# The gated stage of a fused attention, expert and gated-product kernel: other places for the next block's transposes, sums and low parts, and another order of the output's sums

## Chip, cores and metric

The kernel runs on one NeuronCore of a Trainium2 chip, in one launch. The metric is the device time of that launch in microseconds (us); the time before is the median of three runs.

## What is computed

The reference is linear attention, then a mixture of experts with one expert for each token, then a gated product. Cut to what matters here:

```python
q_s = softmax(q, axis=-1); k_s = softmax(k, axis=2)
x = einsum('bhsd,bhde->bhse', q_s, einsum('bhsd,bhse->bhde', k_s, v))     # 4608 tokens x 512
y = gate_w * (relu(x @ w1[e]) @ w2[e])                                   # e = argmax of the gate, for each token
a = y @ w_a                                                              # 512 x 1536
b = y @ w_b                                                              # 512 x 1536
out = (a * b) @ w_out                                                    # 1536 x 512
```

The change lies in the last three lines alone, the gated stage.

## The kernel before

**Blocks, f and steps.** The gated stage takes the 4608 tokens in nine blocks of 512. In a block, a loop runs over `f` = 0 to 11 (128 columns of `w_a` and of `w_b` each). Both products are done at once by a scheme of seven products in place of eight (Strassen's, in Winograd's form), with every operand as a float16 high part and a float16 low part. So `step` (L1792) has seven *steps* for each `f`, and a block has 84, numbered k = 0 to 83. In each step TensorE (PE) first makes one of the products p1, p2, p6, p7, p5, p4, p3 (six matmuls, L1644) into one of two PSUM banks, `x` or `y`, in turn; the banks change their names with each `f`. Then follows one *chunk* of the output product (three matmuls, L1659), taken from a queue (`product()` in `step`).

**Who empties the banks.** p1, p6 and p7 are copied out by ScalarE (ACT; L1803, L1809, L1812). p2, p5 and p4 are added up by VectorE (DVE; L1806, L1815, L1818), p4 is followed by the product `g[:, 1]` (L1819, here *g1*), and p3 is read by the product `g[:, 0]` (L1822, here *g0*). A product can start when the one two steps before has been read out of its bank. From g0 and g1 come the operands of the output product: high parts by ACT (`hi`, L1681), low parts by DVE (`lo`, L1686), sums by GpSimd (POOL; L1695 to L1717). POOL also scales output weights (`scaled`, L1678), twice for each pair of `f`, after every sixth chunk.

**The next block, beside.** While a block is computed, `rows` (L1764) lists by step what is done for the next one: its rows are loaded (step 27, L1306), their peaks are found (`peak`, DVE, L1312), scaled (ACT, L1323), transposed in four *turns* (four PE transposes into the bank that is free, L1328, and one ACT copy out of it, `turned`, L1331), and then made into seven operands A11, A12, A22, S1 to S4: sums by DVE in halves (`add`, L1338), high parts by ACT (L835), low parts by DVE in halves (`lo`, L1348). Where a turn stands, one or two chunks of later steps are done early, so that PE has work while ACT copies.

**The last block's output.** The sums that make the output of the block before (`sum`, L1729) run in steps 1 to 26 of a block: DVE adds the PSUM accumulators p6, p7, p4, p5, p2, p3 one after the other (L1736). The accumulator of p3 is that of p5, which is added to: the chunks of p3 start in step 12.

**Order.** All is written out by hand: each engine takes its instructions in the order in which `step` issues them, which within a step is product, its reader, turn and `turned`, chunks, the operands' `tasks`, the output's `total`, and last what `rows` has put there (`late`).

Of the kernel before, what the change touches and what calls it, by code (L numbers as in the profile page):

```python
# [12 lines left out]
AF = mybir.ActivationFunctionType  # L13
# [23 lines left out]
class Attention:  # L37
# [70 lines left out]
    def rows(self, u):  # L108
        r = 64 * (u // 2 % 2)
        return slice(r, r + 64)  # L110
# [367 lines left out]
def setup_consts(tc, ctx, c):  # L478

    nc = tc.nc  # L480
    cp = ctx.enter_context(tc.tile_pool(name="const", bufs=1))
    c.ident = cp.tile([P, P], F32, name="ident")
    make_identity(nc, c.ident)
    c.two = cp.tile([P, P], F32, name="two")
    nc.gpsimd.memset(c.two, 2.0)
    c.plan = cp.tile([P, 3 * MAXSLOT + 2 * NE + 1], I32, name="plan")
    c.cand = cp.tile([P, 1], I32, name="cand")
    c.pick = cp.tile([P, MAXSLOT, NE], F32, name="pick")
    c.gidx = cp.tile([P, 2 * MAXSLOT], I32, name="gidx")
    c.carry = cp.tile([P, NE], F32, name="carry")  # L490
    nc.gpsimd.memset(c.carry, 0.0)
    c.first = cp.tile([P, NE], F32, name="first")

    def iota(name, n, step=1, base=0):
        t = cp.tile([P, n], F32, name=name)
        nc.gpsimd.iota(t, [[step, n]], base=base, channel_multiplier=0, allow_small_or_imprecise_dtypes=True)
        return t

    c.iota50 = iota("iota50", 2 * MAXSLOT)
    c.is1000 = iota("is1000", 4, base=-1000)  # L500
    c.w8 = iota("w8", NE, -1, NE)
    c.e8 = iota("e8", NE)
# [271 lines left out]
class Work:  # L774
# [20 lines left out]
    def step(self, flush=False):  # L795
        self.now += 1
        for e in self.room:
            self.room[e] = min(self.room[e] + self.STEP, self.STEP)
        for ch in list(self.chains):
            while ch[1] is not None:  # L800
                eng, cost, wait, *cond = ch[1]
                if self.now < ch[2] + wait or (cond and not cond[0]()) or (self.room[eng] < self.LEAST and not flush):
                    break
                self.room[eng] -= cost
                ch[1:] = next(ch[0], None), self.now
            if ch[1] is None:
                self.chains.remove(ch)
# [548 lines left out]
class Gated:  # L1356
# [372 lines left out]
    def sum(self, n):  # L1729

        nc, v, acc, b = self.nc, self.nc.vector, self.acc, self.y[n]
        u = [self.y1.rearrange("p t d -> p (t d)")[:, 512 * i:512 * i + 512].rearrange("p (t c) -> p t c", t=2)
             for i in range(4)]

        def add(o, x, nm, t):
            v.tensor_tensor(u[o][:, t], u[x][:, t], acc[nm][:, t], ALU.add)  # L1736

        def copy(t):
            nc.scalar.copy(u[0][:, t], acc["p1"][:, t])

        def store(t):
            ob = self.ob[t % 2]
            for k in range(2):
                nc.scalar.activation(ob[:, 256 * k:256 * k + 256], u[2 * (t // 2) + k][:, t % 2], AF.Copy, scale=b.fc[:, t:t + 1])
            put = nc.gpsimd.indirect_dma_start(out=self.o[:, :], in_=ob, in_offset=None,
                                               out_offset=bass.IndirectOffsetOnAxis(ap=b.id[:, t:t + 1], axis=0),
                                               bounds_check=NTOK - 1, oob_is_err=False)
            self.tc.declare_no_dep(put.ins, group="out", reason="no two rows have the same token")
            self.tc.add_to_no_dep_group("out", put.ins)

        do = {}
        for f, a, ks in ((copy, (), (1, 2)), (add, (1, 0, "p6"), (6, 7)), (add, (3, 1, "p7"), (8, 8)),
                         (add, (2, 3, "p4"), (10, 10)), (add, (3, 3, "p5"), (11, 11)),
                         (add, (0, 0, "p2"), (17, 21)), (add, (1, 1, "p3"), (23, 24))):
            for t in range(2):
                do.setdefault(ks[t], []).append((f, *a, t))
        for t, k in ((2, 16), (3, 18), (0, 25), (1, 26)):
            do.setdefault(k, []).append((store, t))
        for k in range(27):
            for f, *a in do.get(k, ()):  # L1760
                f(*a)
            yield

    def rows(self, n):  # L1764


        nc, b = self.nc, Rows(self, n, self.y1)
        self.y[n] = b
        late = {}

        def put(s, f, *a):
            late.setdefault(s, []).append(lambda: f(*a))

        put(27, b.load)
        for i, k in enumerate((33, 33, 34, 35, 35, 36, 37, 38)):
            put(k, b.peak, i // 2, slice(i % 2, i % 2 + 1))
        put(39, b.power)
        for t in range(4):
            put(39 + t, b.scale, t)
        turns = {44 + 7 * i: i for i in range(4)}  # L1780
        for j, adds, hi, *lo in ((self.A11, (), 53, 55, 56), (self.S3, (52, 53), 55, 57, 59), (self.A12, (), 67, 68, 69),
                                 (self.A22, (), 68, 70, 71), (self.S1, (66, 67), 69, 71, 72),
                                 (self.S2, (68, 69), 71, 73, 74), (self.S4, (70, 72), 74, 76, 77)):
            for k, at in enumerate(adds):
                put(at, b.add, j, slice(k, k + 1))
            put(hi, b.hi, j, nc.scalar)
            for k in range(2):
                put(lo[k], b.lo, j, slice(k, k + 1))
        put(80, b.factor)
        return b, late, turns  # L1790

    def step(self, n, f, beside):  # L1792


        nc, v = self.nc, self.nc.vector
        a, r, w, u = self.tmp
        g, cf = self.g[f % 2], self.cf[:, f:f + 1]
        i = f // 2
        first = self.A12 if f % 2 else self.A11
        x, y = (t[:, 0:256] for t in (self.banks[f % 2], self.banks[1 - f % 2]))  # L1800

        def p1():
            nc.scalar.copy(w, x)  # L1803

        def p2():
            v.tensor_tensor(a, w, y, ALU.add)  # L1806

        def p6():
            nc.scalar.copy(r, x)  # L1809

        def p7():
            nc.scalar.copy(w, y)  # L1812

        def p5():
            v.tensor_tensor(u, w, x, ALU.add)  # L1815

        def p4():
            v.tensor_tensor(r, r, y, ALU.add)  # L1818
            v.scalar_tensor_tensor(g[:, 1], r, cf, u, ALU.mult, ALU.mult)  # L1819

        def p3():
            v.scalar_tensor_tensor(g[:, 0], x, cf, a, ALU.mult, ALU.mult)  # L1822
            self.hi(i, first, g[:, 0])

        def product():
            next(self.queue, lambda: None)()

        b, late, turns = beside
        for k, use in enumerate((p1, p2, p6, p7, p5, p4, p3)):
            ps = y if k % 2 else x  # L1830
            k += 7 * f
            self.product(n, f, use.__name__, ps)
            use()
            if k in turns:
                b.turn(turns[k], self.banks[1 - f % 2])
                b.turned(turns[k])
                product()
                if f % 2:
                    product()
            if k - 1 not in turns and not (f % 2 and k - 3 in turns):  # L1840
                product()
            next(self.tasks, None)
            next(self.total, None)
            for do in late.get(k, ()):
                do()
# [102 lines left out]
```

## Time and profile before

| | |
|---|---|
| median of the runs | 1457.78 us (1457.41 to 1458.32, 3 runs) |
| the profiled execution: its own time, its span | 1467.53 us, 1465.8 us |
| PE busy | 1366.1 us, 93% of the span |
| DVE busy | 1043.0 us, 71% |
| ACT busy | 674.0 us, 46% |
| POOL busy | 564.2 us, 38% |
| granted TensorE clock, mean over the span | 0.976 |

Shares of busy time are means over the whole kernel, of which the gated stage is the second half, from 652 us on. A busy PE is not PE at its peak, since matmuls overlap and their ends are modelled. The profiled execution took 1467.53 us, 9.75 us more than the median of the runs that were timed without a profile.

### The profile page before, as it was taken

Reading aid. Unit: us, or ns where it says so; the run is one execution under the profiler, and the core shown is the slowest. Engines: PE = TensorE matmul, PEld = TensorE weight load, DVE = VectorE, ACT = ScalarE, POOL = GpSimd, SP = SyncE. Lnnn points to the kernel's source line nnn. Section 1 sums busy time; section 2 is a strip of 40 time slices with the busy share of each in tenths; the row PEclk is TensorE's granted clock in tenths of the full one; section 3 lists DMA queues with packets and bytes.
Section 4 is the critical chain, followed back from the end, with each engine's and each line's share of the span. In section 5 each row is a group of like instructions: output and inputs, shape, how many; then the busy total and the mean of one; then the engine's idle time right before and its main releaser. Section 6 shows DMA issues by size and latency. Waiting matters only on the chain.

```text
span 1465.8 us, 29137 instructions
## 1 busy us (share of the span) xinstructions
PE 1366.1 (93%) x11068; PEld 1112.0 (76%) x11068; DVE 1043.0 (71%) x2340; ACT 674.0 (46%) x1625; POOL 564.2 (38%) x698
## 2 busy tenths in 40 slices
PE   6887898998999999989999999999999999999996
PEld 4776775665576676768888888888888888888885
DVE  5889875875687776426767867777777777767764
ACT  4556554753455454324444444444444444444432
POOL 6755521523334354104343343433334333343433
PEclk9988798999999999999999999999999999999998
DMA  9998245788564345126010010100101001010000
GB/s 240 253 251 220 73 131 164 268 291 271 184 220 140 113 135 165 48 72 255 2 56 4 1 59 1 59 1 16 45 1 59 2 18 42 1 59 1 31 1 30
DMA packets 87919, 145.87 MB, mean 100 GB/s; under 512 B 19792, under 2 KB 60752, under 8 KB 85584
## 3 DMA queue, kind: packets, MB, share of 16 engines
q1 hardware_dynamic: 81136, 123.85, 26.8%
q0 software_dynamic: 6080, 19.95, 4.2%
q8 instruction: 92, 1.51, 0.5%
q14 instruction: 67, 0.55, 0.1%
q10 hardware_dynamic: 544, 0.02, 0.0%
HBM read 149.78 MB, written 46.44 MB: 134 GB/s over the span
## 4 chain that ended last, share of the span: by engine, by line
PE 41%; DVE 10%; issue 2%; ACT 1%; POOL 1%; POOLq 0%; DVEq 0%; ACTq 0%
PE ab L1644 27%; PE mp L1659 13%; DVE raw L1348 1%; DVE y L1338 1%; DVE gp L1686 1%; DVE w L1348 1%; PE ab L1328 1%; DVE ysb L1818 1%; DVE w L1819 1%; DVE xg L1806 1%; DVE g L1819 1%; DVE gu L1815 0%; DVE w L1822 0%; DVE g L1822 0%; DVE y L1736 0%
## 5 line engine op out<-in xcount | busy, mean ns | idle before, releaser
L1644 PEld LDWEIGHTS <-gw 128*128 128x128 f16 x3780 | 369.2, 98 | 60.0 <-issue 13.6
L1644 PE MATMUL ab<-raw,gw 128*128 128x256 f16 x2100 | 280.2, 272 | 5.6 <-ACTq L1267 2.7
L1644 PE MATMUL ab<-w,gw 128*128 128x256 f16 x1680 | 225.2, 273 | 0.8
L1659 PEld LDWEIGHTS <-gp 128*128 128x128 f16 x1944 | 190.8, 98 | 25.9 <-ACT gp L1681 2.1
L1061 PEld LDWEIGHTS <-w 128*128 128x128 f16 x1824 | 180.1, 99 | 38.6 <-issue 12.7
L1061 PE MATMUL ph<-xhl,w 128*128 128x256 f16 x1728 | 198.2, 276 | 9.7 <-issue 4.1
L1078 PE MATMUL py<-w,hh 128*128 128x512 f16 x576 | 172.5, 381 | 2.4 <-DMA w<-wd 2.4
L1659 PE MATMUL mp<-wo,gp 128*128 128x256 f16 x756 | 142.6, 273 | 0.0
L1686 DVE SCALAR_TENSOR_TENSOR gp<-gp,gs 128x256 f16<-128x256 f16 x162 | 81.1, 505 | 59.0 <-ACT gp L1681 58.0
L1069 DVE SCALAR_TENSOR_TENSOR hl<-ph,hh 128x256 f16<-128x256 f32 x144 | 59.2, 420 | 78.7 <-ACT hh L1068 75.6
L1078 PE MATMUL py<-w,hl 128*128 128x512 f16 x288 | 109.9, 382 | 0.0
L1078 PEld LDWEIGHTS <-hh 128*128 128x128 f16 x608 | 59.8, 99 | 64.7 <-issue 4.2
L1460 POOL TENSOR_TENSOR gf<-gf 128x256 f32<-128x256 f32 x72 | 64.5, 916 | 100.4 <-ACT gf L1503 92.0
L1681 ACT ACTIVATE gp<-g 128x256 f16<-128x256 f32 x108 | 45.0, 417 | 115.7 <-DVE g L1822 114.8
L1644 PEld LDWEIGHTS <-w 128*128 128x128 f16 x756 | 73.7, 97 | 29.5 <-issue 21.0
L1717 POOL TENSOR_TENSOR gs<-w 128x256 f32<-128x256 f32 x54 | 39.5, 732 | 134.0 <-DVE w L1822 134.0
L1681 ACT ACTIVATE gp<-w 128x256 f16<-128x256 f32 x54 | 22.5, 417 | 148.9 <-DVE w L1822 146.2
L1659 PE MATMUL mp<-raw,gp 128*128 128x256 f16 x324 | 88.6, 273 | 0.9 <-DVE gp L1686 0.9
L1659 PE MATMUL mp<-w,gp 128*128 128x256 f16 x324 | 88.8, 274 | 0.0
L1068 ACT ACTIVATE hh<-ph 128x256 f16<-128x256 f32 x144 | 54.0, 378 | 74.9 <-PE ph L1061 74.5
L1023 POOL DMA_INDIRECT xg<-xd,gidx x40 | 43.9, 1098 | 106.9 <-ACT xhl L1052 51.4
L1815 DVE TENSOR_TENSOR gu<-tables,ab 128x256 f32<-128x256 f32 x108 | 45.3, 419 | 54.2 <-PE ab L1644 47.1
(337 smaller groups left out, 2798.8 us busy)
## 6 DMA issues: line engine op xcount, KB each, us to landing
w<-wd SPq DMA_DIRECT2D x58, 1024.0 KB
raw<-in_moe_w_dram SPq DMA_DIRECT2D x24, 512.0 KB
yd<-ysb SPq DMA_DIRECT2D x19, 513.0 KB
xd<-x SPq DMA_DIRECT2D x8, 1026.0 KB
y<-yd SPq DMA_DIRECT2D x8, 1026.0 KB
w<-in_k_dram SPq DMA_DIRECT2D x16, 512.0 KB
wd<-wst SPq DMA_DIRECT2D x16, 512.0 KB
g<-in_moe_w_a_dram SPq DMA_DIRECT2D x12, 512.0 KB
```

What stands on the lines that cost most here:

```text
L1023: nc.gpsimd.indirect_dma_start(out=self.x[:, j], out_offset=None, in_=self.xd[0:4 * S if s == 0 else NTOK, :], in_offset=bass.IndirectOffs ...
L1061: nc.tensor.matmul(ph, self.w1[:, w, k, o], x[:, k], start=i == 0, stop=i == 11)
L1068: nc.scalar.activation(self.hh[:, f], ph, AF.Relu)
L1069: nc.vector.scalar_tensor_tensor(self.hl[:, f], ph, 0.0, self.hh[:, f], ALU.max, ALU.subtract)
L1078: nc.tensor.matmul(self.py[j], h[:, f, o], self.w2[:, w, f], start=f == 0 and i == 0, stop=f == 7 and i == 2)
L1460: self.nc.gpsimd.tensor_tensor(s[:, dst], s[:, x], s[:, y], ALU.subtract)
L1644: self.nc.tensor.matmul(ps, self.w[f][:, b, o:o + P], self.y[n].op[:, a, yl, 256 * k:256 * k + 256], start=i == 0 and fresh, stop=i == 5, ...
L1659: self.nc.tensor.matmul(self.acc[nm][:, t], x, y, start=i == t == j == 0 and nm != "p3", stop=i == last and t == 1 and j == 2, skip_group_ ...
L1681: self.nc.scalar.activation(self.part(i, a)[:, 0], x, AF.Copy, scale=2.0 ** -11)
L1686: eng.scalar_tensor_tensor(p[:, 1], p[:, 0], -2048.0, x, ALU.mult, ALU.add)
L1717: pool.tensor_tensor(x, a11, a21, ALU.subtract)
L1815: v.tensor_tensor(u, w, x, ALU.add)
```

## The change

Three tables of step numbers and one order are changed; the same instructions are issued, except that they stand elsewhere. Turns 0 to 3 stand at steps 44, 48, 51, 55 (before 44, 51, 58, 65), and the number of chunks done early beside them is now listed by step. The eight peaks take steps 32 to 38 one or two at a time. The next block's sums, high and low parts take steps 50 to 78 (before 52 to 77, most of them 66 to 77). In the output's sums p5 is added before p4, in step 9, and p4's two halves in steps 11 and 13; the two buffers that hold these results change places in `store`.

```diff
@@ sum
+        c = (u[0], u[1]), (u[3], u[2])
...
-                nc.scalar.activation(ob[:, 256 * k:256 * k + 256], u[2 * (t // 2) + k][:, t % 2], AF.Copy, scale=b.fc[:, t:t + 1])
+                nc.scalar.activation(ob[:, 256 * k:256 * k + 256], c[t // 2][k][:, t % 2], AF.Copy, scale=b.fc[:, t:t + 1])
...
-                         (add, (2, 3, "p4"), (10, 10)), (add, (3, 3, "p5"), (11, 11)),
+                         (add, (2, 3, "p5"), (9, 9)), (add, (3, 3, "p4"), (11, 13)),
@@ rows
-        for i, k in enumerate((33, 33, 34, 35, 35, 36, 37, 38)):
+        for i, k in enumerate((32, 34, 35, 36, 37, 37, 38, 38)):
...
-        turns = {44 + 7 * i: i for i in range(4)}
-        for j, adds, hi, *lo in ((self.A11, (), 53, 55, 56), (self.S3, (52, 53), 55, 57, 59), (self.A12, (), 67, 68, 69),
-                                 (self.A22, (), 68, 70, 71), (self.S1, (66, 67), 69, 71, 72),
-                                 (self.S2, (68, 69), 71, 73, 74), (self.S4, (70, 72), 74, 76, 77)):
+        turns = {44: 0, 48: 1, 51: 2, 55: 3}
+        for j, adds, hi, *lo in ((self.A11, (), 50, 51, 52), (self.S3, (50, 51), 52, 53, 55), (self.A12, (), 57, 58, 59),
+                                 (self.A22, (), 58, 63, 64), (self.S1, (60, 62), 63, 66, 67),
+                                 (self.S2, (65, 65), 66, 70, 72), (self.S4, (69, 73), 74, 77, 78)):
@@ step
+        more, less = ({44: 1, 48: 1, 51: 2, 55: 2}, (45, 49, 52, 54, 56, 58)) if turns else ({}, ())
...
-                product()
-                if f % 2:
+                for _ in range(more[k]):
                     product()
-            if k - 1 not in turns and not (f % 2 and k - 3 in turns):
+            if k not in less:
                 product()
```

In the rows of the changed kernel below, line numbers stand one or two higher (L1736 is L1737, L1803 is L1804), since lines were added above them.

ACT's order in steps 47 to 51, first before and then with the change. `tables` and `ysb` are the copies of p7, p1 and p6, `gs_12767<-gs` is the high part of S4, `gp_12766<-w_92` that of A11, which reads g0; `y_12761<-ab` is the copy that ends a turn, and L835 a high part of the next block.

```order
L1812 COPY tables<-ab_12771 128x256
L1681 ACTIVATE gs_12767<-gs 128x256
L1681 ACTIVATE gp_12766<-w_92 128x256
L1803 COPY tables<-ab_12771 128x256
L1809 COPY ysb<-ab_12771 128x256
L1331 COPY y_12761<-ab_12770 128x4x128
```

```order
L1813 COPY tables<-ab_12771 128x256
L1681 ACTIVATE gs_12767<-gs 128x256
L1681 ACTIVATE gp_12766<-w_92 128x256
L1331 COPY y_12761<-ab_12771 128x4x128
L1804 COPY tables<-ab_12771 128x256
L835 ACTIVATE w_91<-y_12761 128x512
L1810 COPY ysb<-ab_12771 128x256
L1331 COPY y_12761<-ab_12770 128x4x128
```

Turn 1 used to be copied after p6's copy (L1809) in step 51. Now its copy stands in step 48, right behind the high part that reads g0, and turn 2 has the place in step 51.

DVE's order in steps 69 to 74, before and then with the change. L1338 is a half sum of the next block, L1348 a half low part, L1686 a low part of this block's operands; L1822 is g0, L1806 the sum with p2, L1815 the sum with p5.

```order
L1348 TENSOR_TENSOR raw_90<-y_12761,raw_90 128x256
L1338 TENSOR_TENSOR y_12761<-y_12761 128x2x128
L1822 SCALAR_TENSOR_TENSOR g_12763<-ab_12771,gcf,xg 128x256
L1348 TENSOR_TENSOR raw_90<-y_12761,raw_90 128x256
L1338 TENSOR_TENSOR y_12761<-y_12761 128x2x128
L1686 SCALAR_TENSOR_TENSOR gp_12765<-gp_12765,g_12763 128x256
L1348 TENSOR_TENSOR raw_90<-y_12761,raw_90 128x256
L1338 TENSOR_TENSOR y_12761<-y_12761 128x2x128
L1806 TENSOR_TENSOR xg<-tables,ab_12771 128x256
L1686 SCALAR_TENSOR_TENSOR gp_12765<-gp_12765,g_12763 128x256
L1348 TENSOR_TENSOR raw_90<-y_12761,raw_90 128x256 x2
L1686 SCALAR_TENSOR_TENSOR gp_12765<-gp_12765,gs 128x256
```

```order
L1823 SCALAR_TENSOR_TENSOR g_12763<-ab_12771,gcf,xg 128x256
L1338 TENSOR_TENSOR y_12761<-y_12761 128x2x128
L1686 SCALAR_TENSOR_TENSOR gp_12765<-gp_12765,g_12763 128x256
L1348 TENSOR_TENSOR raw_90<-y_12761,raw_90 128x256
L1807 TENSOR_TENSOR xg<-tables,ab_12771 128x256
L1686 SCALAR_TENSOR_TENSOR gp_12765<-gp_12765,g_12763 128x256
L1686 SCALAR_TENSOR_TENSOR gp_12765<-gp_12765,gs 128x256
L1348 TENSOR_TENSOR raw_90<-y_12761,raw_90 128x256
L1686 SCALAR_TENSOR_TENSOR gp_12765<-gp_12765,gs 128x256
```

Between g0 (L1822) and the sum with p2 (L1806) stood five instructions, four of them for the next block and one for this; now there are three, two of them for the next block. Ahead of g0, too, stood two for the next block, and now none.

DVE's order in steps 8 to 12, before and then with the change. L1736 adds an accumulator to the output: `mp7` is p7, `mp4` p4, `mp5` p5.

```order
L1736 TENSOR_TENSOR y1_12761<-y1_12761,mp7_12773 128x256 x2
L1686 SCALAR_TENSOR_TENSOR gp0_12765<-gp0_12765,gs_12764 128x256
L1736 TENSOR_TENSOR y1_12761<-y1_12761,mp4_12775 128x256 x2
L1815 TENSOR_TENSOR gu_12762<-tables_119,ab1_12771 128x256
L1736 TENSOR_TENSOR y1_12761<-y1_12761,mp5_12777 128x256 x2
L1818 TENSOR_TENSOR ysb_94<-ysb_94,ab0_12770 128x256
```

```order
L1737 TENSOR_TENSOR y1_12761<-y1_12761,mp7_12773 128x256 x2
L1737 TENSOR_TENSOR y1_12761<-y1_12761,mp5_12777 128x256 x2
L1686 SCALAR_TENSOR_TENSOR gp0_12765<-gp0_12765,gs_12764 128x256
L1816 TENSOR_TENSOR gu_12762<-tables_119,ab1_12771 128x256
L1737 TENSOR_TENSOR y1_12761<-y1_12761,mp4_12775 128x256
L1819 TENSOR_TENSOR ysb_94<-ysb_94,ab0_12770 128x256
```

Both sums of p5 now stand right behind those of p7, ahead of the low part of step 10 (L1686), and only one half of p4 is left ahead of the sum with p4's product (L1818, now L1819).

## Rows read from the trace of the kernel before

**Rows 1.** Busy us of PE, PEld, DVE, ACT, POOL, then PEclk, DMA; two stretches.
```profile
1002.80:1091.70 88.90, 86.41 (x775) 75.60 (x773) 66.00 (x151) 39.41 (x103) 32.95 (x40) 1.00 0.08 25
...
1075.20:1084.20 9.00, 7.41 (x64) 6.05 (x63) 8.96 (x22) 4.33 (x11) 3.21 (x4) 1.00 0.01 2
```

**Rows 2.** Timeline, steps 11 and 12: start, us, instruction [idle before, releaser].
```profile
1014.74 0.82 PE L1644 MATMUL ab<-raw,gw 128*128 128x256 f16 x6
...
1015.00 0.83 POOL L1678 TENSOR_SCALAR w<-wo 128x768 f16<-128x768 f16 x1 [3.36 <-PE mp L1659]
1015.02 0.74 DVE L1736 TENSOR_TENSOR y<-y,mp 128x256 f32<-128x256 f32 x2
...
1015.82 0.38 PE L1659 MATMUL mp<-wo,gs 128*128 128x256 f16 x2 [0.26 <-DVE y L1736]
```

**Rows 3.** Timeline, steps 33 to 36 of the fifth block.
```profile
1036.65 0.42 DVE L1818 TENSOR_TENSOR ysb<-ysb,ab 128x256 f32<-128x256 f32 x1 [0.49 <-PE ab L1644]
...
1036.78 0.82 PE L1644 MATMUL ab<-raw,gw 128*128 128x256 f16 x6
...
1037.76 0.82 PE L1644 MATMUL ab<-raw,gw 128*128 128x256 f16 x6
...
1037.85 0.74 DVE L1312 TENSOR_REDUCE yh<-y 128x1 f32<-128x256 f32 x2
...
1038.50 0.48 DVE L1822 SCALAR_TENSOR_TENSOR w<-ab,gcf,xg 128x256 f32<-128x256 f32 x1
...
1039.03 0.82 PE L1644 MATMUL ab<-raw,gw 128*128 128x256 f16 x6
```

**Rows 4.** Timeline, where steps 70, 71, 76 and 80 begin, and one DVE row.
```profile
1075.23 0.82 PE L1644 MATMUL ab<-raw,w 128*128 128x256 f16 x6
...
1077.04 0.81 PE L1644 MATMUL ab<-raw,w 128*128 128x256 f16 x6 [0.67 <-DVE g L1822]
...
1078.39 1.04 DVE L1338 TENSOR_TENSOR y<-y 128x256 f32<-128x256 f32 x1
...
1083.36 0.81 PE L1644 MATMUL ab<-raw,w 128*128 128x256 f16 x6 [0.44 <-DVE gu L1815]
...
1087.76 0.81 PE L1644 MATMUL ab<-raw,w 128*128 128x256 f16 x6 [0.32 <-DVE xg L1806]
```

**Rows 5.** Timeline, the turns in steps 51 and 58 of the fifth block.
```profile
1055.38 0.60 PE L1328 MATMUL ab<-ident,y 128*128 128x128 f32 x4
...
1056.02 0.59 ACT L1331 COPY y<-ab 128x512 f32<-128x512 f32 x1
...
1062.04 0.82 PE L1644 MATMUL ab<-raw,gw 128*128 128x256 f16 x6
...
1064.32 1.14 PE L1644 MATMUL ab<-raw,gw 128*128 128x256 f16 x9
```

**Rows 6.** Timeline, steps 48 to 50 of the fifth block.
```profile
1051.61 0.82 PE L1644 MATMUL ab<-raw,gw 128*128 128x256 f16 x6
1051.86 0.83 POOL L1678 TENSOR_SCALAR w<-wo 128x768 f16<-128x768 f16 x1 [2.53 <-PE mp L1659]
1051.94 1.02 DVE L1819 SCALAR_TENSOR_TENSOR w<-ysb,gcf,gu 128x256 f32<-128x256 f32 x1
...
1052.89 0.41 DVE L1686 SCALAR_TENSOR_TENSOR gs<-gs,gs 128x256 f16<-128x256 f16 x1
1053.22 0.47 DVE L1822 SCALAR_TENSOR_TENSOR w<-ab,gcf,xg 128x256 f32<-128x256 f32 x1
...
1053.72 0.42 ACT L1681 ACTIVATE gp<-w 128x256 f16<-128x256 f32 x1 [3.19 <-DVE w L1822]
...
1053.74 0.81 PE L1644 MATMUL ab<-raw,gw 128*128 128x256 f16 x6
```

**Rows 7.** Timeline of SP: the load of the next block's rows is issued.
```profile
1029.81 0.33 SPq L1306 DMA_DIRECT2D y<-yd  x1
```

**Rows 8.** SP's waits in that block: for whom, us in total, times, longest.
```profile
SPq L1306 <- DMA y<-yd: 6.3, 1, 6.3
```

**Rows 9.** Columns as in rows 1: two stretches at the kernel's end.
```profile
1442.40:1445.80 3.40, 1.16 (x10) 0.56 (x7) 2.87 (x4) 1.89 (x7) 2.74 (x4) 1.00 0.00 0
1445.90:1449.20 3.30, 3.22 (x16) 2.31 (x17) 1.86 (x6) 0.19 (x1) 0.83 (x1) 0.50 0.00 0
```

**Rows 10.** Timeline of PE, where the last block's chunks of p3 begin.
```profile
1450.99 0.38 PE L1659 MATMUL mp<-wo,gs 128*128 128x256 f16 x2 [0.85 <-DVE y L1736]
```

## The prediction

> **What bounds it now.** I looked first at the granted clock, then at busy time by stretch, then walked the timeline of the fifth block (1002.78 to 1091.70 us; the second to eighth blocks repeat it to within some 10 ns a step). Over the block PE is busy for 86.41 of 88.90 us at full clock [rows 1]: the stage is a train of products and chunks on PE, and it can only gain where that train halts. A step that nothing delays takes 0.98 us, as from 1036.78 to 1037.76 [rows 3], which is nine matmuls 0.109 apart: 0.655 for the product, 0.33 for the chunk. 84 steps would take 82.5 us; four turns of four transposes add 4 x 0.44. So about 4.6 us a block are halts of PE, and the timeline shows where each stands:
>
> - Step 12, 0.42: its chunk is the first of p3 and adds to the accumulator of p5. It begins at 1015.82, released by DVE's sum (L1736), where the product before it began at 1014.74 and leaves PE free at 1015.40 [rows 2].
> - Steps 35 to 37, 0.29 + 0.17: two peaks (0.74 together) stand ahead of g0, which ends at 1038.98; the next product starts at 1039.03 in place of 1038.74 [rows 3]. A further one delays step 38 likewise.
> - Steps 70 to 80: from 1075.23 to 1087.76 are 12.53 us for ten steps, 9.83 undisturbed, so 2.70 lost; each halt ends with DVE [rows 4], and DVE is busy for 8.96 of 9.00 us there while PE is not [rows 1].
> - Step 58, 0.53: from 1062.04 to 1064.32 are 2.28 [rows 5], while product, transposes and two chunks need 0.655 + 0.44 + 0.655 = 1.75.
> - Step 49, 0.17: p1 to p2 would take 0.98 from 1052.59 and ends only at 1053.74 [rows 6].
> - The turn in step 51 has three chunks beside it: its transposes start at 1055.38, PE has work until 1055.38 + 0.44 + 0.98 = 1056.80, and the copy ends at 1056.61 [rows 5], so nothing is lost. Small halts in steps 7 and 44 make up the rest; the change leaves them as they are.
>
> **The output's sums.** p5 is now summed before p4. DVE has by then ended p7's sums; two sums take 0.74 [rows 2] and fill a stretch in which DVE waits, so p5 is read about 1.9 us earlier than now, well before 1015.40. The p4 halves go into steps 11 and 13, one at a time (0.41), inside the 0.6 us by which DVE's step work may be late. I take the whole 0.42, in each of eight blocks. In the tail PE idles 0.85 for the same sum [rows 10]; behind it stand stores that wait for others, so I count 0.5 there (0 to 0.85).
>
> **The peaks.** The first one moves to step 32, and there the load decides: issued at 1029.81 + 0.33 and waited for 6.3 us by SP's own wait [rows 7, 8], it has landed at 1036.44. DVE would start this peak at about 1036.1, so it now waits, and r + y (L1818, nominally 1036.65 [rows 3]) stands behind it and ends some 0.2 later. The product that waits for r + y starts at 1037.76, so there are 0.5 us left. Behind it g1, a low part and g0 (0.48 + 0.41 + 0.48) end near 1038.5, in time for 1038.74. I allow 0.2 more for the loads of other blocks, which still fits. Then no step has more peaks than its gap holds: 0.46 gained, with 0 and 0.46 as bounds.
>
> **The next block's sums and low parts.** Of its 22 half operations, ten stand now in steps 70 to 79, and five with the change; the rest go to steps 50 to 69, where DVE has room. Walking DVE's queue with the durations of the rows (0.41 for a half beside nothing, 0.95 to 1.04 where a POOL copy runs [rows 4, 6], each 0.08 overlapped), I find two narrow places, steps 61 and 64, and one miss of 0.05. So 2.70 are gained but for 0.1; the other bound is that each of the POOL copies met on the way pushes a reader beyond its slack, 1.2 a block.
>
> What the timeline shows of such a meeting: g1 (L1819) starts at 1051.94, just after POOL's scaling at 1051.86, and takes 1.02 in place of 0.48 [rows 6]; two sums that read PSUM take 0.74 beside the scaling of their step [rows 2], no more than two peaks without one [rows 3]. The Trainium skill (SBUF — State Buffer, Who interferes with whom) says that a VectorE instruction with two inputs in SBUF contends with a GpSimd instruction that reads SBUF, and that reductions never do; by it every moved sum and low part is exposed, and no peak. The trace agrees where it shows both.
>
> **The turns.** Turn 2 takes the place of turn 1 in step 51 and waits as little. The halt of 0.53 at step 58 and the 0.17 at step 49 go. But turns 1 and 3 now stand in steps 48 and 55, each behind p3, and ACT, which takes its instructions in order, has the high part that reads g0 ahead of the turn's copy.
>
> Step 48: p3 starts at 1051.61, the transposes can follow at 1052.27 and two chunks after them, so PE is ready for step 49's p1 at 1051.61 + 0.655 + 0.44 + 0.655 = 1053.36. That p1 writes the bank that the copy empties. g1 meets the scaling and ends at 1052.96, the low part and g0 follow until 1053.69, the high part until 1054.14 [rows 6]; the copy takes 0.59 [rows 5], overlapped by 0.08, and ends near 1054.65. p1 starts at 1054.70: a new wait of 1.33 (1.29 to 1.4 by the overlap; if g1 didn't meet the scaling, 0.79).
>
> Step 55: r + y ends 0.62 into the step (in [rows 3] it ends at 1037.07, 0.29 after p3's start at 1036.78 with a chunk of 0.33 between p4 and p3, and step 54 has no chunk); then g1 0.48, g0 0.47, high part 0.42, copy 0.59, less overlaps: 2.53 after p3's start. PE needs 0.655 + 0.44 + 0.98 = 2.08. A new wait of 0.45.
>
> **Sum for a block.** 0.42 + 0.46 + (2.70 - 0.1) + 0.53 + 0.17 - 1.33 - 0.45 = 2.40 us. Seven blocks: 16.8. The last block has step 12 alone, 0.42, and the tail 0.5. The first has no sums, loses about 1.5 more at step 55 and around it, where its queue of chunks is empty, and gains elsewhere: I take 1.5 (0 to 2.4). Together 19.2 us: the profiled execution would go from 1467.53 to 1448.3, the median from 1457.78 to **1438.6 us**.
>
> **Rivals.**
> - *The wait at step 48 is shorter.* For it speaks that a POOL copy a little later would let g1 go first, 0.54 less in each of eight blocks: 1438.6 - 4.3 = 1434. Against it: the instructions before are the same on PE, DVE and POOL, and the meeting recurs in every block. Were both new waits nothing, it would be 1438.6 - 8 x 1.78 = 1424.
> - *DVE's jam is spread, not ended.* At the bound of 1.2 a block the time is 1438.6 + 8 x 1.1 = 1447. For it: after step 60 the reserves are under 0.1 us twice. Against: DVE has 66.00 busy of 88.90 [rows 1].
> - *The change doesn't do what it says:* the jam costs as much in steps 57 to 68 as now in 70 to 79. Then 8 x 2.6 come back, and the time is 1459, no change. Against: fourteen half operations in steps 66 to 75 become at most nine in any ten steps.
> - *Slower: PE's clock falls at the new wait in step 48.* At the kernel's end PE was busy for 1.16 of 3.40 us at full clock, and ran the next 3.30 us at 0.50, which is 1.2 of 2.4 GHz [rows 9]: one such stretch costs 1.65. One in each block: 1438.6 + 13 = 1452, still faster; it turns slower from 4.8 us at half clock a block, so with two such stretches: 1438.6 + 26 = 1465. Against: PE works on both sides of a wait of 1.33, and the clock stayed full through steps 70 to 80 with 0.67 and more of waits each microsecond or two [rows 1, 4]. The Trainium skill (TensorE: Matmul & The Clock Gate, Part 4: PE-mode transpose) says that transposes do not count as busy for the clock, which would speak for a fall, since four of them stand right before this wait; no row here tells them apart from matmuls in this.
>
> **Chances.** The forecast 0.62, a shorter wait 0.13, a spread jam 0.17, nothing gained 0.04, a clock that falls 0.04 (half of it slower). The range that leaves out no more than two in ten reaches from 1431 (a shorter wait, with 3 us for the tail and the first block) to 1448 (the spread jam). 0.2%, some 3 us, is about what a measurement of this kernel can tell from no change. Faster: 0.62 + 0.13 + 0.17 + 0.02 = 0.94; same 0.03; slower 0.03.
>
> **What would show it.** In the changed profile, blocks of about 86.5 us; step 12's chunk without a wait; no product released late by g0 in steps 35 to 38; in steps 70 to 80 products 0.98 apart; a wait of PE of about 1.3 us ended by ACT's copy (L1331) once a block in step 49, and one of 0.45 in step 56. I am wrong if PE waits for DVE between steps 57 and 68 by more than 0.3 in sum, if p1 in step 49 starts less than 0.8 after PE is ready, if the load makes L1819 (before L1818) in step 33 end over 0.5 late, or if the clock shows 0.5 anywhere in the stage.

## The result and the profile after

The changed kernel takes 1437.72 us (median of 4 runs, 1435.67 to 1440.36) where the kernel before, run beside it, takes 1457.6 us (4 runs, 1456.6 to 1458.32). The ratio is 0.9865, with a 95% interval of 0.9844 to 0.9886: faster by some 20 us.

The page of the profiled execution, its span, the busy time of each engine and the clock row in 40 slices:

```profile
span 1434.0 us, 29107 instructions
...
PE 1345.8 (94%) x11068; PEld 1105.8 (77%) x11068; DVE 1052.4 (73%) x2340; ACT 674.9 (47%) x1625; POOL 563.8 (39%) x698
...
PEclk9998899999999999999999999999999999999999
```

The two profiled spans differ by 31.8 us, more than the medians, and only part of that is the change's. The gated stage begins at 652.1 us in the profile before and at 640.0 us in the one after; the work ahead of it is the same in both, and in the ten profiled executions of all kernels but the one before it ended between 637.9 and 643.1 us. That is 12.1 us. The stage itself went from 813.7 to 793.9 us: 19.8 us, which is what the medians show and what the working spoke of (19.2).

Busy time by stretch, columns as in [rows 1]: the fifth block, nine microseconds of its steps 70 to 78, the stage's first 2.9 us, and the stage from there to behind PE's last work.

```profile
982.95:1069.54 86.59, 85.16 (x774) 75.65 (x772) 67.44 (x151) 39.44 (x103) 32.97 (x40) 1.00 0.08 26
1055.20:1064.20 9.00, 9.00 (x85) 8.07 (x84) 8.20 (x18) 4.20 (x11) 4.06 (x6) 1.00 0.01 2
640.02:642.90 2.88, 2.88 (x14) 2.08 (x15) 0.05 (x1) 0.37 (x1) 0.00 (x0) 0.50 0.22 74
642.90:1428.00 785.10, 764.56 (x6920) 677.25 (x6918) 591.59 (x1314) 347.26 (x911) 301.69 (x368) 1.00 0.10 36
```

Against [rows 1] the block is 2.3 us shorter (the second to eighth blocks take 86.49 to 86.59, before 88.9), and in the 9 us where PE stood still for 1.59 and DVE for 0.04, it is now PE that never stops, while DVE has 0.80 to spare. The clock is full from 642.9 us on. In the 2.9 us before, with which the stage begins, it is at half (0.50); PE had been busy for 2.26 of the 5.02 us ahead of them.

The waits of PE in that block, summed: who waits for whom, us, times, longest. Before, four groups stood here, all for DVE: the sum with p2 (L1806), g0 (L1822), the sum with p5 (L1815) and the output's sum (L1736).

```profile
PE ab L1644 <- DVE xg L1806: 0.7, 2, 0.4
PE ab L1644 <- DVE g L1822: 0.7, 1, 0.7
PE ab L1644 <- DVE gu L1815: 0.4, 1, 0.4
PE mp L1659 <- DVE y L1736: 0.3, 1, 0.3
```

None of them is left, and one has come:

```profile
PE ab L1644 <- ACT y L1331: 1.4, 2, 1.2
```

Where it stands is seen in the timeline of steps 48 and 49, which answers to [rows 6] (columns as in [rows 2]):

```profile
1031.00 0.82 PE L1644 MATMUL ab<-raw,gw 128*128 128x256 f16 x6
1031.25 0.83 POOL L1678 TENSOR_SCALAR w<-wo 128x768 f16<-128x768 f16 x1 [2.34 <-PE mp L1659]
1031.33 1.03 DVE L1820 SCALAR_TENSOR_TENSOR w<-ysb,gcf,gu 128x256 f32<-128x256 f32 x1
...
1032.62 0.47 DVE L1823 SCALAR_TENSOR_TENSOR w<-ab,gcf,xg 128x256 f32<-128x256 f32 x1
...
1033.12 0.42 ACT L1681 ACTIVATE gp<-w 128x256 f16<-128x256 f32 x1 [3.20 <-DVE w L1823]
...
1033.44 0.57 ACT L1331 COPY y<-ab 128x512 f32<-128x512 f32 x1
...
1034.06 0.81 PE L1644 MATMUL ab<-raw,gw 128*128 128x256 f16 x6 [1.16 <-ACT y L1331]
```

It reads from bottom to top: p1 of step 49 (1034.06) waited for the turn's copy, the copy stood in ACT's queue behind the high part, the high part waited for g0, and g0 stood behind a g1 that took 1.03 beside POOL's scaling. PE would have been ready at 1031.00 + 1.75 = 1032.75, so the wait is 1.31.

Step 12 and the peaks, in two stretches of the timeline, answer to [rows 2, 3]:

```profile
993.33 0.74 DVE L1737 TENSOR_TENSOR y<-y,mp 128x256 f32<-128x256 f32 x2
...
994.91 0.82 PE L1644 MATMUL ab<-raw,gw 128*128 128x256 f16 x6
...
995.56 0.38 PE L1659 MATMUL mp<-wo,gs 128*128 128x256 f16 x2
...
1016.08 0.42 DVE L1312 TENSOR_REDUCE yh<-y 128x1 f32<-128x256 f32 x1 [0.18 <-DMA y<-yd]
...
1016.42 0.41 DVE L1819 TENSOR_TENSOR ysb<-ysb,ab 128x256 f32<-128x256 f32 x1
...
1017.51 0.82 PE L1644 MATMUL ab<-raw,gw 128*128 128x256 f16 x6
...
1018.49 0.82 PE L1644 MATMUL ab<-raw,gw 128*128 128x256 f16 x6
```

The sum of p5 is done at 994.07, and the chunk that needs it starts at 995.56, as soon as its product lets it: no bracket, no wait. The first peak waits 0.18 for its load and r + y (1016.42) stands behind it, but the products of steps 35 and 36 keep 0.98 apart.

Further down one small wait is new. In steps 78 and 79:

```profile
1063.26 0.73 POOL L1717 TENSOR_TENSOR gs<-w 128x256 f32<-128x256 f32 x1 [3.00 <-DVE w L1823]
...
1063.60 0.67 DVE L1686 SCALAR_TENSOR_TENSOR gp<-gp,w 128x256 f16<-128x256 f16 x1 [0.48 <-ACT gp L1681]
1063.95 1.01 POOL L1678 TENSOR_SCALAR raw<-ysb 128x768 f16<-128x768 f16 x1
...
1064.19 1.04 DVE L1348 TENSOR_TENSOR w<-y,w 128x256 f16<-128x256 f32 x1
...
1064.52 0.82 PE L1644 MATMUL ab<-raw,w 128*128 128x256 f16 x6
...
1065.15 0.41 DVE L1807 TENSOR_TENSOR xg<-tables,ab 128x256 f32<-128x256 f32 x1
...
1065.61 0.82 PE L1644 MATMUL ab<-raw,w 128*128 128x256 f16 x6
```

A low part of the last sum S4 (L1348) meets POOL's scaling, takes 1.04, and makes the sum with p2 late; the next product comes 1.09 behind the one before in place of 0.98.

In the tail the chunks of p3 that waited 0.85 in [rows 10] now wait 0.20:

```profile
1418.95 0.38 PE L1659 MATMUL mp<-wo,gs 128*128 128x256 f16 x2 [0.20 <-DVE y L1737]
```

### The profile page after: what moved, and what is told of

Read it like the earlier page. It is cut to its first block, busy times and chain, and to the rows that moved or that the text cites. A ratio compares the mean times of both kernels' runs of the same rounds, so it can differ in the third digit from the quotient of the medians.

```text
span 1434.0 us, 29107 instructions
## 1 busy us (share of the span) xinstructions
PE 1345.8 (94%) x11068; PEld 1105.8 (77%) x11068; DVE 1052.4 (73%) x2340; ACT 674.9 (47%) x1625; POOL 563.8 (39%) x698
## 4 chain that ended last, share of the span: by engine, by line
PE 49%; DVE 3%; ACT 2%; issue 1%; POOL 1%; POOLq 0%; DVEq 0%; ACTq 0%
PE ab L1644 33%; PE mp L1659 15%; ACT y L1331 1%; DVE w L1820 1%; ACT gp L1681 1%; DVE ysb L1819 1%; PE ab L1328 0%; DVE g L1820 0%; DVE g L1823 0%; ACT y L1323 0%; DVE w L1823 0%; DVE gs L1686 0%; POOL out_dram L1746 0%; DVE w L1348 0%; DVE gp L1686 0%
## 5 line engine op out<-in xcount | busy, mean ns | idle before, releaser
L1061 PEld LDWEIGHTS <-w 128*128 128x128 f16 x1824 | 179.4, 99 | 37.3 <-issue 12.2
L1686 DVE SCALAR_TENSOR_TENSOR gp<-gp,gs 128x256 f16<-128x256 f16 x162 | 87.3, 543 | 32.5 <-ACT gp L1681 32.3
L1686 DVE SCALAR_TENSOR_TENSOR gp<-gp,g 128x256 f16<-128x256 f16 x108 | 74.2, 688 | 15.7 <-ACT gp L1681 15.7
L1810 ACT COPY ysb<-ab 128x256 f32<-128x256 f32 x108 | 40.2, 372 | 92.7 <-PE ab L1644 92.2
```

The source lines that it names most:

```text
L1061: nc.tensor.matmul(ph, self.w1[:, w, k, o], x[:, k], start=i == 0, stop=i == 11)
L1686: eng.scalar_tensor_tensor(p[:, 1], p[:, 0], -2048.0, x, ALU.mult, ALU.add)
```

## The experiments

The theory is that of the prediction: five separate halts of PE are gone, and two new waits have come whose length is the chain g1, low part, g0, high part, copy, with ACT's order and one meeting of g1 and POOL in it. The rivals: the turns cost nothing by themselves and the gain is less than the halts said; or the new wait is that of the transposes and the bank, whatever ACT's order is. Three kernels make one part of the change alone, and six change something in the changed kernel. The time given for a block is that of most of the second to eighth blocks in the profile of that run, from first product to first product.

**The order of the output's sums alone** (on the kernel before):

```diff
...
-                         (add, (2, 3, "p4"), (10, 10)), (add, (3, 3, "p5"), (11, 11)),
+                         (add, (2, 3, "p5"), (9, 9)), (add, (3, 3, "p4"), (11, 13)),
...
```

> The kernel before, with p5 summed before p4 in the output's sums, all else as before. Theory: step 12 takes 0.98 in place of 1.40 in blocks 2 to 9, a block 88.48 in place of 88.91, all other steps as they were, and the idle stretch of PE before the first chunk of p3 in the tail shrinks from 0.85 to 0.2 or less. Rival (the wait moves to another reader, step 10 or 13): block unchanged.

Measured: 1449.92 us in one run (before on the same chip 1455.72), and the block 88.49 (before 88.91): 0.42 less, with no wait in step 12 and none before the first chunk of p3 in the tail. What the rows of that step said is what it was worth. (The block carries this, not the time of one run: the runs of the kernel before reach from 1451.46 to 1460.72 on that chip.)

**The peaks alone** (on the kernel before):

```diff
-        for i, k in enumerate((33, 33, 34, 35, 35, 36, 37, 38)):
+        for i, k in enumerate((32, 34, 35, 36, 37, 37, 38, 38)):
```

> The kernel before, with the eight peaks at steps 32, 34, 35, 36, 37, 37, 38, 38, all else as before. Theory: the load lands in time, steps 35 and 37 take 0.98 in place of 1.27 and 1.15, a block 88.45 in place of 88.91, and the first peak in step 32 waits for the load without delaying PE. Rival (the first peak waits for the load and holds up the reader of p4 behind it): a halt of PE in step 34 or 35, and a block at 88.7 or above.

Measured: 1452.44 us in one run (before on the same chip 1454.02), block 88.45, that is 0.46 less; here too the block carries it. The load is what the first peak waits for, and it costs nothing; in the timeline of DVE:

```profile
1023.47 0.42 DVE L1312 TENSOR_REDUCE yh<-y 128x1 f32<-128x256 f32 x1 [0.49 <-DMA y<-yd]
```

**The turns alone** (the changed kernel with the peaks, the sums and low parts, and the output's order as before):

```diff
@@ rows
-        turns = {44 + 7 * i: i for i in range(4)}
+        turns = {44: 0, 48: 1, 51: 2, 55: 3}
@@ step (the chunks, as in the change)
...
```

> The kernel before, with the four turns at 44, 48, 51, 55 and their chunks, all else as before. Theory: the turns alone cost time: 1.31 + 0.45 of new waits against 0.53 (step 58) and 0.17 (step 49) saved, so a block takes about 89.9 to 90.0 us in place of 88.91, steps 70 to 80 stay at 12.5, and the time rises by 7 to 9 us. Rival (the earlier turns are themselves a gain, or free): block at 88.9 or below.

Measured: 1463.25 us (7 runs, 1460.38 to 1464.67), ratio 1.0041 (1.002 to 1.0061), block 89.90. The turns by themselves make the kernel slower, by 0.99 a block and 7.5 us in all, as expected; steps 70 to 80, expected at 12.5, take 12.21. The waits of PE in the fifth block:

```profile
PE ab L1644 <- ACT y L1331: 1.4, 2, 1.2
PE ab L1644 <- DVE xg L1806: 0.7, 2, 0.4
PE ab L1644 <- DVE gu L1815: 0.4, 1, 0.4
PE ab L1644 <- DVE g L1822: 0.3, 1, 0.3
PE mp L1659 <- DVE y L1736: 0.3, 1, 0.3
```

The new wait for the copy has its full 1.4 here too, so it comes from the turns and from nothing else in the change; DVE's groups are those of before, but for 0.4 less at g0.

The sums and low parts can't be tried without the turns: they read rows that the turns of before transpose only later. Their part is what is left: 88.91 + 0.99 - 0.42 - 0.46 - 86.49 = 2.53 us a block. That is worked out, not run.

**The turn's copy ahead of the high part** (on the changed kernel, as are all that follow). ACT's order in steps 48 and 55, nothing else:

```diff
@@ p3
-            self.hi(i, first, g[:, 0])
@@ step
                 b.turned(turns[k])
+            if use is p3:
+                self.hi(i, first, g[:, 0])
+            if k in turns:
                 for _ in range(more[k]):
```

> The changed kernel, with the turn's ACT copy ahead of the high part that reads g0 in steps 48 and 55; nothing else moves. My theory (the two new waits, 1.31 and 0.42 us a block, are ACT's order: the copy stands behind a high part that waits for g0): the wait before step 49's p1 falls to about 0.2, that in step 56 to nothing, and a block takes 84.9 to 85.3 us in place of 86.49; the time falls by 10 to 12 us. Rival (the waits come from DVE or from the bank, whatever ACT's order): the block stays at 86.5 and the time does not move. Second rival (the waits were the slack that let DVE work off the next block's sums): what is gained in steps 49 and 56 comes back as waits for DVE in steps 57 to 70, block above 86.

Measured: 1426.19 us (1423.83 to 1427.27), ratio 0.98 (0.9776 to 0.9824), block 85.00, so 1.49 less than the changed kernel's. Timeline of step 48:

```profile
1026.67 0.83 POOL L1678 TENSOR_SCALAR w<-wo 128x768 f16<-128x768 f16 x1 [2.34 <-PE mp L1659]
1026.75 1.03 DVE L1820 SCALAR_TENSOR_TENSOR w<-ysb,gcf,gu 128x256 f32<-128x256 f32 x1
...
1027.71 0.59 ACT L1331 COPY y<-ab 128x512 f32<-128x512 f32 x1 [2.37 <-PE ab L1328]
...
1028.35 0.49 PE L1644 MATMUL ab<-raw,gw 128*128 128x256 f16 x3
1028.54 0.42 ACT L1681 ACTIVATE gp<-w 128x256 f16<-128x256 f32 x1 [0.24 <-DVE w L1823]
```

g1 is as slow as before, yet the copy is now released by PE's own transposes, and p1 starts at 1028.35, 0.18 behind its earliest 1028.17 in place of 1.31. Step 55 takes 2.15, so 0.07 of the wait before step 56's p1 is left, where none was expected. Nothing came back in steps 57 to 70, so the waits weren't slack that DVE needed. That the bank and the transposes set the wait is refuted; it was ACT's order.

**POOL's scaling issued one chunk later:**

```diff
@@ pairs
-                self.scaled((i + 1) % n, k // 3)
+                self.held.append(((i + 1) % n, k // 3))
@@ step, product
+            held, self.held = self.held, []
             next(self.queue, lambda: None)()
+            for h in held:
+                self.scaled(*h)
```

> The changed kernel, with each of POOL's weight scalings issued one chunk later, so that it does not run beside g1 in steps 6 and 48. Theory (half of a microsecond of the wait in step 49, and the 0.17 in step 7, come from g1 meeting that scaling): g1 takes 0.48 in place of 1.03 in step 48, the wait in step 49 falls from 1.31 to about 0.8, step 7 takes 0.98, block 85.8 us. Rival (POOL's scaling has no part in it; the wait is the chain g0, high part, copy alone): the wait stays at 1.3. The scalings will meet other DVE instructions one step later; if those stand ahead of a reader without slack, a wait of up to 0.5 appears there instead.

Measured: 1435.9 us (1433.55 to 1438.01), ratio 0.9865 (0.9841 to 0.9888), block as in the changed kernel. The timeline tells why:

```profile
1033.54 0.83 POOL L1678 TENSOR_SCALAR w<-wo 128x768 f16<-128x768 f16 x1 [2.33 <-PE mp L1659]
1033.61 1.03 DVE L1820 SCALAR_TENSOR_TENSOR w<-ysb,gcf,gu 128x256 f32<-128x256 f32 x1
```

In step 48 the scaling starts at the same place, 0.26 after p3 (1033.28), since no other instruction of POOL stood between its old place and its new one, and what releases it is a chunk of PE that hadn't moved. So the edit decides nothing about g1: a miss of the design. Elsewhere it did move POOL's work: in steps 0, 30, 42 and 72 of the second to ninth blocks the scaling now follows one or two sums that it used to precede, and the blocks stay at 86.49. In the first block it did so in step 70, and step 72 takes 1.24 in place of 1.50; this bears on the first block's term below.

**The same, two chunks later,** so that the scaling stands in POOL's queue behind the sum S3, which waits for g0:

```diff
@@ pairs
-                self.scaled((i + 1) % n, k // 3)
+                self.held.append([2, (i + 1) % n, k // 3])
...
```

> The changed kernel, with each weight scaling of POOL issued two chunks later, so that in steps 6 and 48 it stands behind POOL's sum S3 in its queue and cannot run beside g1. (The run before moved the issue by one chunk, which left it in the same place of POOL's queue.) Theory: g1 takes 0.48 in place of 1.03 in both places; the wait in step 49 falls from 1.31 to 0.76, step 7 takes 0.98, so a block takes about 85.8 us in place of 86.49. Rival (g1 is slow there for another reason): g1 stays at 1.03 and the block at 86.5. Where the scaling now meets other DVE instructions a halt of up to 0.5 may appear.

Measured: 1431.63 us (1426.56 to 1432.76), ratio 0.9834 (0.9811 to 0.9858), block 85.78. Step 48 (L1827 is g1, L1830 g0, L1724 S3):

```profile
1030.60 0.82 PE L1644 MATMUL ab<-raw,gw 128*128 128x256 f16 x6
1030.93 0.48 DVE L1827 SCALAR_TENSOR_TENSOR w<-ysb,gcf,gu 128x256 f32<-128x256 f32 x1
...
1032.29 0.72 POOL L1724 TENSOR_TENSOR gs<-w 128x256 f32<-128x256 f32 x1 [3.77 <-DVE w L1830]
...
...
1032.98 1.00 POOL L1678 TENSOR_SCALAR w<-wo 128x768 f16<-128x768 f16 x1
1033.12 0.38 PE L1644 MATMUL ab<-raw,gw 128*128 128x256 f16 x2 [0.61 <-ACT y L1331]
```

With POOL out of the way g1 takes 0.48, and p1 starts 2.52 after p3 in place of 3.06: 0.54 less, the price that the prediction put on this meeting. The other 0.17 of the block is step 7, where the same meeting made a small halt. The Trainium skill (SBUF — State Buffer, Summary: rules for kernel authors) states that when a VectorE instruction has two inputs in SBUF while a GpSimd instruction reads SBUF, the one that comes second is blocked until the first is done. The trace agrees: in the changed kernel g1 ends 0.28 after the scaling does (1032.36 and 1032.08), and here, alone, it takes 0.48.

**Both edits,** the copy first and the scaling two chunks later:

> The changed kernel with the turn's copy ahead of the high part and the scaling two chunks later. Theory: with the copy ahead, g1 is no longer on the path to step 49's p1, so the later scaling is worth only step 7: a block takes 84.83 us (85.00 with the copy alone), the time falls by 1 to 1.5 us against the run with the copy alone. If both gains added up in full, the block would take 84.3 us.

Measured: 1421.52 us (1417.22 to 1424.94), ratio 0.9774 (0.9747 to 0.9801), block 84.83. The two don't add: once the copy no longer waits for g0, a faster g1 gives nothing in step 48, and only step 7's 0.17 is left of it. The time is 4.7 us below the 1426.19 with the copy alone, where 1 to 1.5 were expected, but the two ran on different chips (before 1454.02 and 1455.72). In their profiles the stage is 3.3 us shorter: 1.2 in seven blocks, 0.86 in the first, and 1.22 in the last block and the tail, where the kernel with the copy alone has a stretch at half clock.

**The copy first, and the last low parts one step later,** against the wait in step 79:

```diff
-                                 (self.S2, (65, 65), 66, 70, 72), (self.S4, (69, 73), 74, 77, 78)):
+                                 (self.S2, (65, 65), 66, 70, 72), (self.S4, (69, 73), 74, 78, 79)):
```

> The changed kernel with the turn's copy ahead of the high part, and the two low parts of S4 in steps 78 and 79 in place of 77 and 78. Theory: the halt of 0.11 in step 79 comes from the first of them, which meets POOL's scaling and stands ahead of the sum with p2; behind that sum it costs nothing, and a block takes 84.89 us in place of 85.00. Rival: the halt only moves to step 80 or 81.

Measured: 1420.59 us (1420.25 to 1422.69), ratio 0.9773 (0.9756 to 0.9789), block 84.89; the 0.11 of step 79 is gone.

**All three edits:**

> The changed kernel with three edits together: the turn's copy ahead of the high part in steps 48 and 55, POOL's scaling behind the copies of the next sums, and the last four sums' low parts one step later (steps 78 and 79). Theory (the three waits are separate, in steps 48, 55 and 79, and what is left of each adds up): a block of 84.72 us, that is 0.11 less than the two edits without the low parts (84.83), and a time 0.8 us below that kernel's 1421.5, some 1420.7. Rival (the low part, moved past the scaling that now stands later in POOL's queue, meets it again, and a wait stays at step 79 or appears at step 0): a block of 84.8 to 85.0 and no gain over it.

Measured: 1421.23 us (5 runs, 1419.58 to 1422.96), ratio 0.976 (0.9741 to 0.9779), block 84.72. The busy time of its fifth block, measured to the start of the sixth (columns as in [rows 1]):

```profile
975.67:1060.48 84.81, 84.73 (x774) 75.64 (x772) 65.18 (x151) 39.25 (x103) 33.36 (x41) 1.00 0.08 26
```

PE is busy for 84.73 of 84.81 us (this block has 0.1 more than the others, as in the changed kernel). The block came out as expected; that the whole is 0.8 us faster than with two edits can't be told from these runs (1421.23 against 1421.52 and 1420.59, on more than one chip). Against the kernel before on the same chip (1454.02, 1454.02 and 1456.09) these three versions save 32.5, 33.4 and 34.9 us where the changed kernel saves 19.9, so they are 13 to 15 us better.

## Why the prediction was right, point by point

The time (1437.72, forecast 1438.6) came out close, and most terms with it, but the first block's term was off in both of its parts, and something that is not in the sum hid that in the profiles.

- **The output's sums,** 0.42 a block: 0.42, alone and in the whole.
- **The peaks,** 0.46: 0.46. The wait for the load came (0.18 here, 0.49 in the kernel with the peaks alone), r + y stood behind it, and the slack of 0.5 that the working counted for PE held.
- **Sums and low parts,** 2.70 less 0.1: steps 70 to 80 now take 9.93 in place of 12.53, so 2.60 less, and from the second block on nothing is late in steps 57 to 78. The 0.1 is there, but in another place: the narrow places at steps 61 and 64 held, while step 79 lost 0.11 by a meeting with POOL. Worked out from the kernels with one part, it is worth 2.53: with the turns alone, step 70 halts 0.33 less and step 61 halts 0.26, so that 0.07 of the gain is theirs. One count of the working is off by one: steps 58 to 67 hold ten half operations, not "at most nine"; no product was late there.
- **Step 58 and step 49,** 0.53 + 0.17: both gone.
- **The new wait in step 49,** 1.33: 1.31, and each link of its chain was in the trace. The kernel with the copy first leaves 0.18 of it, the one with POOL later shortens it by 0.54.
- **The new wait in step 56,** 0.45: step 55 takes 2.52 where 2.08 are needed, so 0.44.
- **A block,** 2.40 less: 2.42 (88.91 to 86.49), the one with an odd 0.1 in steps 43 and 44 set aside.
- **The first block,** 1.5 less (0 to 2.4): 0.50 (83.95 to 83.45), inside the bounds, but by other amounts than the working's. The terms of the other blocks without step 12 come to 1.98; "about 1.5 more" lost leaves 0.48, so 1.0 of the 1.5 must be the "gains elsewhere", for which no row of this block is shown. What the steps gain by the change (us, a loss with a minus):

| steps | first block | fifth block |
|---|---|---|
| 0 to 13 | -0.22 | 0.42 (step 12) |
| 35 to 37 | 0.84 | 0.46 |
| 48 to 59 | -1.49 | -1.49 |
| 60 to 69 | 0.06 | 0.44 |
| 70 to 83 | 1.32 | 2.60 |

  So the further loss of 1.5 didn't come: steps 55 and 56 lose 0.31 more than in the fifth block, and 57 to 59 gain as much more. What is missing is the gain in the jam: steps 70 to 83 halted for only 2.12 before, not 2.70, and 0.79 of it is left. These are the two parts of the working that failed, one in each direction. The first row says nothing of the change: this block begins at half clock here, and with the output's order alone, which begins so too, it loses 0.20 there; at full clock these steps lose 0.13 with the turns alone and gain 0.16 with the scaling one chunk later.

  Most of the 0.79 is step 72, which takes 1.50 and waits for the sum with p2 (L1807). In its trace three instructions of DVE ahead of that sum meet POOL, one after the other, and take 1.08, 0.94 and 0.94:

```profile
709.82 0.83 POOL L1678 TENSOR_SCALAR w<-hl 128x768 f16<-128x768 f16 x1 [4.14 <-PE mp L1659]
709.85 1.08 DVE L1338 TENSOR_TENSOR y<-y 128x256 f32<-128x256 f32 x1
...
710.62 0.89 POOL L1695 TENSOR_TENSOR gs<-w,g 128x256 f32<-128x256 f32 x1
710.85 0.94 DVE L1686 SCALAR_TENSOR_TENSOR gp<-gp,g 128x256 f16<-128x256 f16 x1
...
711.71 0.94 DVE L1348 TENSOR_TENSOR w<-y,w 128x256 f16<-128x256 f32 x1
```

  In the fifth block POOL's scaling stands two steps later, behind the sums, and step 72 takes 0.98. The kernel with the scaling one chunk later puts it behind both sums in the first block too, the first of the three takes 0.72, and step 72 takes 1.24: half of its halt is the scaling's place. In the other half the scaling meets the last of the three (1.04); a kernel without that meeting was not run.
- **The tail,** 0.5 (0 to 0.85): 0.48. The kernel with the turns alone has the old order of the sums and the same last block otherwise; from the last block's start to the end it takes 105.84, the changed kernel 104.94, which is 0.42 for step 12 and 0.48.
- **What hid the miss:** the last block and the tail of the profile before took 107.42, so 2.48 more than after, not 0.92. The rest, near 1.6, is the stretch at half clock in [rows 9]: in the changed kernel's tail the clock stays full until PE's last work. It is not the change's work in any simple way: the turns alone had no fall either (its last block and tail take 105.84, 1.58 less than before, with the same steps in the block), while the kernels with the sums' order alone, with the peaks alone and with the copy first had one. Without it the stage would have gained 18.2, some 1.0 below the sum. So the agreement of the two profiles with the sum (19.8 and 19.2) is in part luck. How the 19.9 us between the medians divide is not on record: the execution profiled before (1467.53) is not one of the timed runs.

Of the rivals, the shorter wait did not come by itself, but the kernel with POOL's scaling behind S3 shows that its price (0.54) was right; the spread jam and "nothing gained" are refuted by steps of 0.98 from 57 to 78 (0.65 in step 58, which has no chunk) in the second to eighth blocks. The clock did not fall at the new wait: four transposes, two chunks and then 1.31 of idle PE stand in each of eight blocks, and the granted clock is 1.00, of the two levels the 2.4 GHz one, from 642.9 to 1428.0. The sign "if the clock shows 0.5 anywhere in the stage" did come, in the stage's first 2.9 us, but ahead of every turn: the kernel with the output's order alone has such a start too, those with the turns alone and the peaks alone have none, and what decides it is open. The Trainium skill (TensorE: Matmul & The Clock Gate, Part 4: PE-mode transpose) says that transposes don't count as busy for the clock in the same way; a fall that would follow from it is not in this trace, and whether they count was not measured.

## What to carry to other kernels

Walk each in-order queue past the moved instruction: what the turns cost was no work of PE but one copy that stood behind an instruction with a late operand on ACT, and changing the order of those two was worth 1.49 us in each block, more than half of what the whole change gave. A gain must be counted at every place where its neighbours differ (here the first block, where POOL's scaling falls on other steps), and a total that fits doesn't prove its terms: split the two traces by stage before believing it. An edit that issues an instruction later moved it in time only where that put something that waits ahead of it in its own engine's queue; look at the trace whether it moved before reading the time.

## What the runs showed of the hardware

- DVE and POOL can push each other back and forth: in the rows of steps 78 and 79 above a low part of DVE (L1686) ends 0.28 behind POOL's sum (0.67 in place of 0.41), POOL's scaling behind it then takes 1.01 in place of 0.83, and DVE's next low part, which starts in the scaling, takes 1.04 and ends 0.27 behind it. From the second block on, all 205 DVE instructions with two operands in SBUF (L1338, L1348, L1686 and g1) that start inside a POOL scaling or sum, at least 0.32 before its end, end 0.27 to 0.29 behind it, whether they take 0.41 alone or 0.48; sums that read one operand from PSUM (L1737, L1807) keep their 0.41 there. What such a meeting costs thus goes by what is left of POOL's instruction, and a POOL instruction that starts behind it can be late in turn.
- An idle PE of 1.31 us in each block of 86.5 did not lower the clock, while in the tail of the kernel before it fell after a stretch in which PE was busy for 1.16 of 3.40 us [rows 9]. In the changed kernel's tail PE idles for the same 1.83 and 0.59 us, and the clock stays full; which tails fall differs from kernel to kernel (see above) and was not settled.
